# Gated linear attention and routed experts on one core: attention outputs computed turned, on halves and quarters of TensorE's array, and expert inputs turned on TensorE

## The chip, the cores and the metric

The kernel runs on one core of a Trainium2 chip. A core has five engines that work side by side, each through its own list of instructions in order: TensorE (PE: matrix products; its loads of the stationary operand are listed as PEld), VectorE (DVE), ScalarE (ACT), GpSimd (POOL) and SyncE (SP, which issues most DMAs here). TensorE writes to PSUM; VectorE and ScalarE read it from there. The metric is the device time of one execution in microseconds, as the median of several runs.

## The reference

Two layers follow each other. The first is a recurrence over 768 time steps, for 4 batches of 8 heads of width 48:

```python
state = alpha[:, :, t, :, None] * state + np.einsum('bhd,bhe->bhde', k[:, :, t], v[:, :, t])
y[:, :, t] = np.einsum('bhd,bhde->bhe', q[:, :, t], state)
```

(that is, the state decays by `alpha` in each key dimension, takes up the outer product of `k` and `v`, and is read by `q`). The 8 heads of a token laid side by side are its row `x` of 384 numbers, 3072 rows in all. The second layer sends each row to one of 8 experts:

```python
logits = x @ w_gate + modality_bias[modality_id]
e_idx = np.argmax(logits, axis=1)          # gate_w: softmax weight of that expert
h = np.maximum(x[mask] @ w1[e], 0.0)       # 384 -> 1024
out[mask] = gate_w[mask, None] * (h @ w2[e])
```

Everything is fp32.

## The kernel before

**Attention.** The tokens are cut into 24 pieces of 128 (6 per batch). One turn of the main loop (lines 666 to 705) is a step: it loads a piece, turns `alpha`, `k` and `q` on TensorE (`trans`, line 218: four 128x128 transposes for each, two heads padded to 64 rows each in one transpose), makes the running products of `alpha` forward and backward by two scans on VectorE (G, line 231; Fw, line 238), scales keys and queries with them (kh, qh: lines 254, 257), and then works in three stages of a software pipeline: `decay` of piece s, `scale` of piece s-1, `scores` of piece s-2, `combine` of piece s-3. `scores` (line 266) makes the 128x128 score blocks of 8 heads, each from 48 rows, into `sc`; ScalarE copies them out and GpSimd zeroes the upper triangle (line 271).

`combine` (lines 281 to 318) makes the output. The state that enters a piece is S; scaled, it is laid by ScalarE into `UB` (U), two heads of a pair on the diagonal of a 128x96 block with zeros elsewhere. The state's update `kv` (line 298) uses halves of the array: 64 output rows per head. The output `y` has tokens on the partitions and 384 columns. For each of the 4 head pairs there are three products with 96 columns: the turned queries qh (128 rows by 128 tokens, the stationary operand) with U (line 309), and for each of the two heads the turned scores (stationary) with `v`, padded by zero columns to the pair's 96 (line 312). That is 12 products a piece, 8 in the first piece of a batch, where there is no state. Each fp32 product is two records in the trace. ScalarE copies `y` to `xs` and SP sends it to the table `xd` in memory. `logits_pe` (line 320) then turns `xs` (three transposes, line 324), ScalarE copies the result to `xc`, and three products with 8 columns each (line 329) make the logits.

**Routing.** Groups of pieces are routed while the attention goes on (`route_group`, `route_early`), and the rest after the last piece (`route_end`, lines 496 to 540): a chain of small VectorE instructions with a few TensorE products between them, whose end is a table of row numbers by expert (lines 537, 445). Rows of one expert fill slots of 256.

**Experts.** `experts` (line 713) works through 12 full slots and, behind branches, a last part that in this data is one `half` (line 803). A slot gathers 256 rows of `xd` by index (GpSimd, line 577) and loads its expert's w1 and w2 (SP, lines 553, 555). To get more than the plain precision of the fast format, each operand is split in a rounded high part (ScalarE) and a low part that holds the rest (`split`, line 741: `eng.tensor_tensor` on VectorE, or for w2 of slot 0 and quarters 0 and 2 of w2 in every slot on GpSimd, line 772), and each product is three: high by high, low by high, high by low (lines 764 to 766 and 785 to 787). A slot is 72 products with 256 columns, 48 with 384. `prep` (line 721) turns the gathered rows: for slot 1 by six TensorE transposes, for the others by 16 32x32-block transposes on VectorE (line 737) into `xf`, from which ScalarE and VectorE make the high and low part (lines 738, 739). Slot 0's first layer (line 111) is done in plain fp32 between the routing's instructions.

What order each engine has is decided by a scheduler that simulates the program; `issue_after` holds some instructions back behind others. Few tiles limit it: `tr` has three PSUM buffers, `sc` two, `kv`, `y` and `rt` one.

Of the kernel before, what the change touches and what calls it, by code (L numbers as in the profile page):

```python
# [8 lines left out]
F32 = mybir.dt.float32  # L9
# [38 lines left out]
NTURN = 2  # L48
W2POOL = (0, 2)
# [7 lines left out]
def attention_moe(ctx: ExitStack, tc: tile.TileContext, q, k, v, alpha, mid, wg, mb, w1, w2, out):  # L57
# [28 lines left out]
    for i in range(NV):  # L86
        t = ac.tile([P, 2 * H + 1, D], F32, name=f"vt{i}")
        VT.append(t)
        pool.memset(t[:, 0::2], 0.0)
# [38 lines left out]
    def load(i, names="akqv"):  # L128
        b, c = divmod(i, NC)
        for n, t in (("a", alpha), ("k", k), ("q", q), ("v", v)):  # L130
            if n in names:
                dst = VT[i % NV][:, 1::2] if n == "v" else nat[n, i % NB][:, :, :D]
# [49 lines left out]
    pool.tensor_scalar(rev, iof[:, :E], -1.0, float(E), op0=ALU.mult, op1=ALU.add)  # L182
    ones = cp.tile([P, P], BF16, name="ones")
# [97 lines left out]
    def combine(i):  # L281
# [3 lines left out]
        if c > 0:  # L285
            S0 = st[i, "S"]
            A = st[i, "G"][:, 1::SEG].unsqueeze(2).broadcast_to([P, NP, D])
            t1 = sb.tile([P, NP, D], F32, name="t1")
            vec.tensor_tensor(t1, S0, A, op=ALU.mult)
            for g in range(2):  # L290
                r = slice(64 * g, 64 * g + 64)
                act.copy(U[r, :, g * D : (g + 1) * D], t1[r])
        if c < NC - 1:
            kn = st[i, "n"]
            kv = ps.tile([P, NP, D], F32, name="kv")
            for h in range(H):
                r = slice(64 * (h % 2), 64 * (h % 2) + 64)
                pe.matmul(kv[r, h // 2], kn[:, h // 2, r], vt[:, 2 * h + 1], start=True, stop=True)  # L298
# [6 lines left out]
        y = ps.tile([P, DM], F32, name="y")  # L305
        for j in range(NP):
            yj = y[:, 2 * D * j : 2 * D * (j + 1)]
            if c > 0:
                pe.matmul(yj, qh[:, j], U[:, j], start=True, stop=False)  # L309
            for g in range(2):  # L310
                z = 4 * j + 1 + g
                pe.matmul(  # L312
                    yj, sc[g][:, j], vt[:, z : z + 2].rearrange("p a b -> p (a b)"), start=(c == 0 and g == 0), stop=(g == 1)
                )
        xs = sb.tile([P, DM], F32, name="xs", bufs=4)
        act.copy(xs, y)
        sp.dma_start(xd[row(i) : row(i) + P, :], xs)
        st[i, "x"] = xs

    def logits_pe(i, xs, pl, after=None):  # L320
        xt = ps.tile([P, ND, P], F32, name="tr", bufs=3)
        with issue_after(after):
            for c in range(ND):
                mark["logitst"] = pe.transpose(xt[:, c], xs[:, c * P : (c + 1) * P], ident)  # L324
        xc = pl.tile([P, ND, P], F32, name="xc")
        mark["xc"] = act.copy(xc, xt)
        lp = ps.tile([P, E], F32, name="kv")
        for c in range(ND):
            mark["logits"] = pe.matmul(lp, xc[:, c], wgs[:, c], start=(c == 0), stop=(c == ND - 1))
# [336 lines left out]
    for s in range(NU + 4):  # L666
# [22 lines left out]
        if 0 <= s - 3 < NU:  # L689
# [3 lines left out]
            logits_pe(s - 3, st[s - 3, "x"], sb, ("step", ND - 1) if s - 3 == NU - 1 else None)  # L693
# [19 lines left out]
    def experts(ahead):  # L713
# [7 lines left out]
        def prep(i):  # L721
            x = xg[i % NX]
            xH, xL = XH[i % 2], XL[i % 2]
            if i < NTURN:
                for name, d0, d1 in (("kv", 0, 2), ("y", 2, 3)):
                    xp = ps.tile([P, d1 - d0, T], F32, name=name)
                    for d in range(d0, d1):
                        for u in range(2):
                            pe.transpose(xp[:, d - d0, u * P : (u + 1) * P], x[:, u, d * P : (d + 1) * P], ident)
                    act.copy(xH[:, d0:d1], xp)  # L730
                    vec.tensor_tensor(xL[:, d0:d1], xp, xH[:, d0:d1].bitcast(F32), op=ALU.subtract)
                return
            src = x.rearrange("p u (c a d) -> p a u c d", c=ND, a=4)
            dst = xf.rearrange("p c (u b t) -> p b u c t", u=2, b=4)
            for a in range(4):
                for b in range(4):
                    vec.transpose(dst[32 * a : 32 * (a + 1), b], src[32 * b : 32 * (b + 1), a])  # L737
            act.copy(xH, xf)
            vec.tensor_tensor(xL, xf, xH.bitcast(F32), op=ALU.subtract)

        def split(name, src, eng=vec):
# [3 lines left out]
            eng.tensor_tensor(lw, src, hi.bitcast(F32), op=ALU.subtract)  # L745
            return hi, lw

        def layer1(i):
# [5 lines left out]
            for j in range(4):  # L754
# [17 lines left out]
                w2s.append(split("w2", W2[:, 2 * j : 2 * j + 2], pool if plain or j in W2POOL else vec))  # L772
# [67 lines left out]
        def tail(i):  # L840
            if i < NS:
                with tc.If(ns > i):
                    with tc.If(nfl > i) as full:
                        ahead_of(i + 1)
                        slot(i)
# [65 lines left out]
```

## Time and profile before

| what | value |
|---|---|
| runs before | 463.2, 461.2, 463.09 us; median 463.09 us |
| the profiled execution's own time | 465.73 us |
| its span, first to last instruction | 464.0 us |
| mean granted TensorE clock in it | 0.954 |
| busy: PE, DVE, ACT, POOL | 410.2, 347.0, 229.1, 190.6 us |
| first to last transposes of a piece of `alpha` | 4.3 to 167 us |
| second layer of slot 0 begins | 219.8 us |
| last full slot ends, half slot begins | 432.6 us |
| last product of the half slot begins | 443.1 us |

A timeline row gives start, length, engine, line, operation, tiles (written <- read), shapes and how many; the length reaches to the end of the last one, which for TensorE includes its latency, so that the pace is read from one row's start to the next row's. A square bracket at the end is the engine's idle time before and what ended it. In a row of the windows view stands the stretch, its length, and for each engine busy time and number of instructions, then the granted clock (1.00 is full), the share of the DMA engines and GB/s.

### The profile page before, as it was taken

What the parts mean: (1) busy time and instruction counts of PE and PEld (TensorE: products, weight loads), DVE (VectorE), ACT (ScalarE), POOL (GpSimd) and SP (SyncE); (2) the same over time, 40 slices, a digit from 0 to 9 for tenths busy, and PEclk for the clock granted to TensorE, in tenths of its full rate; (3) what the DMA queues carried; (4) which work ended last, traced back from release to release, by engine and by line L of the source; (5) the groups of instructions that cost most, each with busy time, mean ns of one, the idle gap of its engine ahead of it and who ended that gap; (6) DMA issues with size and microseconds to landing.
All of it is one profiled execution on the core that took longest, in us unless ns stands there. A gap on an engine that the chain in (4) does not pass through costs nothing.

```text
span 464.0 us, 9508 instructions
## 1 busy us (share of the span) xinstructions
PE 410.2 (88%) x3432; PEld 390.1 (84%) x3432; DVE 347.0 (75%) x817; ACT 229.1 (49%) x419; POOL 190.6 (41%) x204
## 2 busy tenths in 40 slices
PE   4999999999999999987978797889999999999920
PEld 3889989898898888865968697899999999999910
DVE  7867777678769982458899999988978988932450
ACT  3565654656464445154645364536656665532410
POOL 9321212112121444043839775647657634720410
PEclk9999999999999999597999899989999999999975
DMA  8989764667465874000996564756586567472200
GB/s 162 198 182 198 170 140 102 134 141 165 89 144 106 290 249 172 19 17 9 383 340 192 203 216 160 270 188 209 188 302 210 184 250 264 134 223 99 65 18 5
DMA packets 134267, 78.76 MB, mean 170 GB/s; under 512 B 103489, under 2 KB 120958, under 8 KB 134200
## 3 DMA queue, kind: packets, MB, share of 16 engines
q1 hardware_dynamic: 129912, 67.70, 52.0%
q0 software_dynamic: 4288, 10.24, 6.4%
q8 instruction: 32, 0.52, 0.5%
q14 instruction: 35, 0.29, 0.2%
HBM read 68.48 MB, written 9.65 MB: 168 GB/s over the span
## 4 chain that ended last, share of the span: by engine, by line
PE 57%; DVE 23%; issue 8%; ACT 4%; POOL 3%; DMA 2%; SPq 0%; POOLq 0%; DVEq 0%; ACTq 0%
PE y L312 6%; PE sc L266 5%; PE sc L787 5%; PE sc L786 5%; PE sc L785 5%; PE tr L221 5%; PE tr L764 5%; PE tr L766 5%; PE tr L765 5%; DVE xf L737 4%; DVE G L231 3%; DVE Fw L238 3%; PE y L309 3%; PE kv L298 2%; PE tr L324 2%
## 5 line engine op out<-in xcount | busy, mean ns | idle before, releaser
L764 PE MATMUL tr<-xH,w1H 128*128 128x256 f32 x264 | 76.3, 289 | 12.8 <-DVE hL L770 10.6
L271 POOL TENSOR_SCALAR_AFFINE_SELECT scT<-scT 128x512 f32<-128x512 f32 x48 | 31.6, 680 | 123.2 <-ACT scT L270 123.2
L766 PE MATMUL tr<-xH,w1L 128*128 128x256 f32 x264 | 75.7, 287 | 0.0
L765 PE MATMUL tr<-xL,w1H 128*128 128x256 f32 x264 | 75.5, 286 | 0.0
L737 DVE STREAM_TRANSPOSE xf<-xg 32x192 f32<-32x192 f32 x192 | 71.0, 370 | 4.0 <-DMA xg<-xd,idx 1.2
L745 POOL TENSOR_TENSOR w2L<-w2r,w2H 128x768 fp32r<-128x768 f32 x26 | 48.2, 1862 | 61.6 <-ACT w2H L743 44.4
L787 PE MATMUL sc<-w2H,hL 128*128 128x384 f32 x192 | 61.7, 337 | 2.6 <-DVE hL L770 2.6
L764 PEld LDWEIGHTS tr<-xH,w1H 128*128 128x128 f32 x264 | 51.7, 196 | 14.4 <-issue 14.4
L785 PE MATMUL sc<-w2H,hH 128*128 128x384 f32 x192 | 63.6, 336 | 0.0
L786 PE MATMUL sc<-w2L,hH 128*128 128x384 f32 x192 | 63.3, 335 | 0.0
L312 PE MATMUL y<-vt,scT 128*128 128x96 f32 x384 | 60.5, 280 | 0.0
L745 DVE TENSOR_TENSOR w1L<-w1r,w1H 128x768 fp32r<-128x768 f32 x44 | 50.2, 1150 | 11.9 <-ACT w1H L743 11.7
L743 ACT CAST w1H<-w1r 128x768 fp32r<-128x768 f32 x44 | 36.3, 833 | 43.5 <-PE tr L765 27.1
L743 ACT CAST w2H<-w2r 128x768 fp32r<-128x768 f32 x52 | 42.7, 832 | 28.2 <-PE sc L787 16.2
L312 PEld LDWEIGHTS y<-vt,scT 128*128 128x128 f32 x384 | 52.3, 197 | 0.2
L765 PEld LDWEIGHTS tr<-xL,w1H 128*128 128x128 f32 x264 | 51.7, 196 | 0.0
L766 PEld LDWEIGHTS tr<-xH,w1L 128*128 128x128 f32 x264 | 51.6, 195 | 0.0
L577 POOL DMA_INDIRECT xg<-xd,idx x28 | 37.7, 1347 | 29.7 <-DVE xf L737 13.3
L770 DVE SCALAR_TENSOR_TENSOR hL<-tr,hH 128x512 fp32r<-128x512 f32 x48 | 32.8, 684 | 10.5 <-ACT hH L768 10.4
L787 PEld LDWEIGHTS sc<-w2H,hL 128*128 128x128 f32 x192 | 35.9, 188 | 3.8 <-DVE hL L770 3.8
L791 POOL DMA_INDIRECT out_dram<-os,odx x24 | 27.2, 1133 | 25.6 <-issue 11.0
L768 ACT ACTIVATE hH<-tr 128x512 fp32r<-128x512 f32 x48 | 28.5, 594 | 18.0 <-PE tr L766 9.4
(216 smaller groups left out, 851.0 us busy)
## 6 DMA issues: line engine op xcount, KB each, us to landing
w1r<-in_moe_w_dram SPq DMA_DIRECT2D x28, 768.0 KB
w2r<-in_moe_w_dram SPq DMA_DIRECT2D x28, 768.0 KB
nat_a<-in_alpha_dram SPq DMA_DIRECT2D x24, 192.0 KB
nat_k<-in_k_dram SPq DMA_DIRECT2D x24, 192.0 KB
nat_q<-in_q_dram SPq DMA_DIRECT2D x24, 192.0 KB
vt<-in_v_dram SPq DMA_DIRECT2D x24, 192.0 KB
xd<-xs SPq DMA_DIRECT2D x24, 192.0 KB
xg<-xd,idx POOLq DMA_INDIRECT x28
```

The source lines that it names most:

```text
L312: pe.matmul(yj, sc[g][:, j], vt[:, z : z + 2].rearrange("p a b -> p (a b)"), start=(c == 0 and g == 0), stop=(g == 1))
L577: pool.indirect_dma_start(xg[i % NX][:, u], None, xd[0:rows], ix, bounds_check=rows - 1, oob_is_err=False)
L737: vec.transpose(dst[32 * a : 32 * (a + 1), b], src[32 * b : 32 * (b + 1), a])
L743: act.copy(hi, src)
L745: eng.tensor_tensor(lw, src, hi.bitcast(F32), op=ALU.subtract)
L764: pe.matmul(hp[:, z], wH[:, d, fs], xH[:, d], start=(d == 0), stop=False)
L765: pe.matmul(hp[:, z], wH[:, d, fs], xL[:, d], start=False, stop=False)
L766: pe.matmul(hp[:, z], wL[:, d, fs], xH[:, d], start=False, stop=(d == ND - 1))
L770: vec.scalar_tensor_tensor(hL, hp, 0.0, hH.bitcast(F32), op0=ALU.max, op1=ALU.subtract)
L785: pe.matmul(op, hH[:, z, us], wH[:, z], start=(f == 0), stop=False)
L786: pe.matmul(op, hH[:, z, us], wL[:, z], start=False, stop=False)
L787: pe.matmul(op, hL[:, z, us], wH[:, z], start=False, stop=(f == NF - 1))
```

## The change

`y` is made turned. For each head pair and each of its two heads, a product has 64 output rows (half of the array's columns): U's 64 columns of that head, or the head's `v` padded from 48 to 64 columns, is now the stationary operand, and the queries or the scores (128 tokens) stream. A piece has 16 such products, 8 in a batch's first piece. ScalarE copies the turned output (512 columns) to `yt`. From `yt` two things are made: `rows` turns it back on TensorE (four transposes), ScalarE drops the padding, and SP sends it to `xd`; `logits` multiplies it with a padded `w_gate`, four products with 32 output rows each, on quarters of the array (the four head pairs' shares), ScalarE copies these, and one product with `sel8` adds the four shares. In the experts `prep` turns every slot's rows on TensorE and ScalarE and VectorE make the high and low parts straight from PSUM, and every low part of w2 is made on VectorE. The old `logits_pe` stays for a fallback path that isn't run.

```diff
-        t = ac.tile([P, 2 * H + 1, D], F32, name=f"vt{i}")
+        t = ac.tile([P, H, 64], F32, name=f"vt{i}")
...
+    wgp = ac.tile([P, NP, 32], F32, name="wgp")
+    pool.memset(wgp, 0.0)
+    for g in range(2):
+        sp.dma_start(wgp[64 * g : 64 * g + D, :, :E], wg.rearrange("(j g d) e -> g d j e", g=2, d=D)[g])
...
-        t = ac.tile([P, NP, 2 * D], F32, name=f"UB{i}")
+        t = ac.tile([P, NP, 2, 64], F32, name=f"UB{i}")
...
+    sel8 = ac.tile([P, E], F32, name="sel8")
+    pool.tensor_copy(sel8, ident[:, :E])
+    for j in range(1, NP):
+        pool.tensor_tensor(sel8, sel8, ident[:, 32 * j : 32 * j + E], op=ALU.add)
...
-        y = ps.tile([P, DM], F32, name="y")
+        y = ps.tile([P, NP, P], F32, name="y")
         for j in range(NP):
+            halves = [slice(64 * g, 64 * g + 64) for g in range(2)]
             if c > 0:
-                pe.matmul(yj, qh[:, j], U[:, j], start=True, stop=False)
-            for g in range(2):
-                z = 4 * j + 1 + g
-                pe.matmul(
-                    yj, sc[g][:, j], vt[:, z : z + 2].rearrange("p a b -> p (a b)"), start=(c == 0 and g == 0), stop=(g == 1)
+                for g, r in enumerate(halves):
+                    pe.matmul(y[r, j], U[:, j, g], qh[:, j], start=True, stop=False)
+            for g, r in enumerate(halves):
+                pe.matmul(y[r, j], vt[:, 2 * j + g], sc[g][:, j], start=(c == 0), stop=True)
+        yt = sb.tile([P, NP, P], F32, name="yt")
+        mark["yt"] = act.copy(yt, y)
...
+    def rows(i):
+        p = ps.tile([P, NP, P], F32, name="tr", bufs=3)
+        for j in range(NP):
+            pe.transpose(p[:, j], st[i, "y"][:, j], ident)
...
+        sp.dma_start(xd[row(i) : row(i) + P, :], xs)
+    def logits(i, after=None):
+        lt = ps.tile([P, P], F32, name="kv")
+        with issue_after(after):
+            for j in range(NP):
+                mark["logitst"] = pe.matmul(
+                    lt[32 * j : 32 * j + 32], wgp[:, j], st[i, "y"][:, j], start=True, stop=True
+                )
+        ls = sb.tile([P, P], F32, name="lts")
+        mark["xc"] = act.copy(ls, lt)
+        lp = ps.tile([P, E], F32, name="kv")
+        mark["logits"] = pe.matmul(lp, ls, sel8, start=True, stop=True)
...
-            for a in range(4):
-                for b in range(4):
-                    vec.transpose(dst[32 * a : 32 * (a + 1), b], src[32 * b : 32 * (b + 1), a])
-            act.copy(xH, xf)
-            vec.tensor_tensor(xL, xf, xH.bitcast(F32), op=ALU.subtract)
...
-                w2s.append(split("w2", W2[:, 2 * j : 2 * j + 2], pool if plain or j in W2POOL else vec))
+                w2s.append(split("w2", W2[:, 2 * j : 2 * j + 2]))
```

The scheduler orders the engines anew. TensorE in a step of the attention, before: L329 the logits, L221 transposes of a piece, L276 the turned keys, L309 and L312 the output, L298 the state, L266 the scores, L324 the logits' transposes.

```order
L329 MATMUL kv<-wgs,xc 128x8 x3
L221 MATMUL tr<-ident,nat_q_80 128x128 x4
L276 MATMUL tr<-ident,kh 128x128 x4
L312 MATMUL y<-vt_104,scT 128x96
L298 MATMUL kv<-vt_104,knat 64x48 x8
L266 MATMUL sc<-qh,kh 128x128 x8
L324 MATMUL tr<-ident,xs 128x128 x3
L221 MATMUL tr<-ident,nat_a_88 128x128 x4
L221 MATMUL tr<-ident,nat_k_84 128x128 x4
L309 MATMUL y<-UB_154,qh 128x96
```

The same place now: L341 the four shares of the logits, L228 transposes of a piece, L318 and L320 the output, L283 the turned keys, L347 the sum of the shares. Behind these rows follow three more output products, the scores, the state, and the transposes of `rows`.

```order
L341 MATMUL kv<-yt,wgp 32x128 x4
L228 MATMUL tr<-ident,nat_q_86 128x128 x4
L318 MATMUL y<-qh,UB_158 64x128
L283 MATMUL tr<-ident,kh 128x128 x4
L318 MATMUL y<-qh,UB_158 64x128
L320 MATMUL y<-scT,vt_106 64x128 x2
L318 MATMUL y<-qh,UB_158 64x128 x2
L320 MATMUL y<-scT,vt_106 64x128 x2
L318 MATMUL y<-qh,UB_158 64x128 x2
L320 MATMUL y<-scT,vt_106 64x128 x2
L318 MATMUL y<-qh,UB_158 64x128
L347 MATMUL kv<-sel_183,lts 128x8
```

The output's products (64 rows) are cut twice by products on the whole array (128 rows): by the turned keys and by the sum of the shares. Before, only the state and the scores left the whole array, and they stood side by side.

VectorE among the experts' slots, before (L737 turns a slot's rows, L739 its low part, L745 low parts of weights, L770 low part of the hidden layer):

```order
L739 TENSOR_TENSOR xL_2885<-xf,xH_2883 128x768
L745 TENSOR_TENSOR w2L<-w2r_113,w2H 128x768
L737 STREAM_TRANSPOSE xf<-xg_116 32x2x3x32 x16
L745 TENSOR_TENSOR w2L<-w2r_115,w2H 128x768
L745 TENSOR_TENSOR w1L<-w1r_114,w1H 128x768
L770 SCALAR_TENSOR_TENSOR hL<-tr,hH 128x512
```

And now (L761 the low part from PSUM, L769 weights, L794 hidden layer):

```order
L794 SCALAR_TENSOR_TENSOR hL<-tr,hH 128x512
L761 TENSOR_TENSOR xL_3118<-kv,xH_3116 128x512
L761 TENSOR_TENSOR xL_3118<-y,xH_3116 128x256
L769 TENSOR_TENSOR w1L<-w1r_114,w1H 128x768
L794 SCALAR_TENSOR_TENSOR hL<-tr,hH 128x512
L769 TENSOR_TENSOR w2L<-w2r_113,w2H 128x768 x2
L769 TENSOR_TENSOR w2L<-w2r_115,w2H 128x768 x2
```

The 16 block transposes are gone from VectorE's list, and four low parts of w2 stand there in each slot where two stood. On TensorE six transposes stand in each slot between the third and the fourth quarter of its first layer. GpSimd's list keeps its gathers and output writes and has no `w2L` any more.

More of the change, by code (lines that the diff above doesn't have):

```diff
@@ L47 @@
 AFLOOR = 1.0e-30
-NTURN = 2
-W2POOL = (0, 2)
 STEPS = (("key", 21), ("key0", 20), ("count", 9), ("rank", 8), ("logits", 6), ("logitst", 4))
@@ L131, in load @@
             if n in names:
-                dst = VT[i % NV][:, 1::2] if n == "v" else nat[n, i % NB][:, :, :D]
+                dst = VT[i % NV][:, :, :D] if n == "v" else nat[n, i % NB][:, :, :D]
                 sp.dma_start(dst, t[b, :, c * P : (c + 1) * P, :].rearrange("h t d -> t h d"))
@@ L291, in combine @@
                 r = slice(64 * g, 64 * g + 64)
-                act.copy(U[r, :, g * D : (g + 1) * D], t1[r])
+                act.copy(U[r, :, g, :D], t1[r])
         if c < NC - 1:
@@ L297, in combine @@
                 r = slice(64 * (h % 2), 64 * (h % 2) + 64)
-                pe.matmul(kv[r, h // 2], kn[:, h // 2, r], vt[:, 2 * h + 1], start=True, stop=True)
+                pe.matmul(kv[r, h // 2], kn[:, h // 2, r], vt[:, h, :D], start=True, stop=True)
             S1 = sb.tile([P, NP, D], F32, name="S")
@@ L315, in combine @@
[L315 to L320, printed above, removed]
+                for g, r in enumerate(halves):
[3 more added lines that the diff above has]
+        yt = sb.tile([P, NP, P], F32, name="yt")
@@ L321, in logits_pe @@
+    def logits_pe(i, xs, pl):
         xt = ps.tile([P, ND, P], F32, name="tr", bufs=3)
-        with issue_after(after):
-            for c in range(ND):
-                mark["logitst"] = pe.transpose(xt[:, c], xs[:, c * P : (c + 1) * P], ident)
+        for c in range(ND):
+            pe.transpose(xt[:, c], xs[:, c * P : (c + 1) * P], ident)
         xc = pl.tile([P, ND, P], F32, name="xc")
-        mark["xc"] = act.copy(xc, xt)
+        act.copy(xc, xt)
         lp = ps.tile([P, E], F32, name="kv")
@@ L328, in logits_pe @@
         for c in range(ND):
-            mark["logits"] = pe.matmul(lp, xc[:, c], wgs[:, c], start=(c == 0), stop=(c == ND - 1))
+            pe.matmul(lp, xc[:, c], wgs[:, c], start=(c == 0), stop=(c == ND - 1))
         vec.tensor_tensor(L[:, i], lp, bt[:, i], op=ALU.add)
@@ L692, in attention_moe @@
                 hp0 = first_steps()
-            logits_pe(s - 3, st[s - 3, "x"], sb, ("step", ND - 1) if s - 3 == NU - 1 else None)
+            logits(s - 3, ("step", ND - 1) if s - 3 == NU - 1 else None)
+            rows(s - 3)
             for after, t0, t1 in GROUPS:
@@ L723, in prep, with split @@
             xH, xL = XH[i % 2], XL[i % 2]
[L724 to L729, printed above, removed]
+            for name, d0, d1 in (("kv", 0, 2), ("y", 2, 3)):
+                xp = ps.tile([P, d1 - d0, T], F32, name=name)
+                for d in range(d0, d1):
+                    for u in range(2):
+                        pe.transpose(xp[:, d - d0, u * P : (u + 1) * P], x[:, u, d * P : (d + 1) * P], ident)
+                if i < NS0:
                     act.copy(xH[:, d0:d1], xp)
                     vec.tensor_tensor(xL[:, d0:d1], xp, xH[:, d0:d1].bitcast(F32), op=ALU.subtract)
-                return
-            src = x.rearrange("p u (c a d) -> p a u c d", c=ND, a=4)
-            dst = xf.rearrange("p c (u b t) -> p b u c t", u=2, b=4)
-            for a in range(4):
-                for b in range(4):
[L737 to L741, printed above, removed]
+                else:
+                    act.copy(xf[:, d0:d1], xp)
+        def split(name, src):
             hi = wp.tile(list(src.shape), F32R, name=name + "H")
@@ L844, in tail @@
                         ahead_of(i + 1)
+                        act.copy(XH[i % 2], xf)
+                        vec.tensor_tensor(XL[i % 2], xf, XH[i % 2].bitcast(F32), op=ALU.subtract)
                         slot(i)
```

10 lines of the change are left out of this document (7 added, 3 removed).

## The prediction

> **What bounds the kernel now.** I read busy time in windows first, then the order of time on TensorE (PE) inside a step, then who waits for whom. Two stretches of the experts, the first four full slots behind slot 0 and six later ones (start, length, then busy us of PE, its loads, DVE, ACT, POOL):
>
> ```profile
> 228.47:313.94 85.47, 72.28 (x480) 69.93 (x480) 80.78 (x138) 42.46 (x63) 53.40 (x40) 0.96 0.68 229
> 313.94:415.62 101.68, 101.68 (x721) 101.68 (x721) 84.09 (x150) 59.79 (x87) 58.02 (x43) 1.00 0.66 221
> ```
>
> A slot is 120 products, so the second row is six slots of 101.68 / 6 = 16.95 us, PE never idle: the pace PE can hold. Four slots at that pace are 67.8 us; the first row took 85.47. So 17.7 us are lost there, with DVE busy 80.78 of 85.47. DVE is what PE waits for:
>
> ```profile
> PE tr L764 <- DVE hL L770: 10.6, 4, 3.4
> ```
>
> Why DVE is late is seen on DVE and POOL side by side, here at 231:
>
> ```profile
> 230.00 0.96 DVE L745 TENSOR_TENSOR w2L<-w2r,w2H 128x768 fp32r<-128x768 f32 x1 [1.09 <-ACT w2H L743]
> 231.37 5.01 DVE L745 TENSOR_TENSOR w1L<-w1r,w1H 128x768 fp32r<-128x768 f32 x1 [0.40 <-ACT w1H L743]
> 236.31 1.88 DVE L737 STREAM_TRANSPOSE xf<-xg 32x192 f32<-32x192 f32 x5
> ...
> 231.89 3.67 POOL L745 TENSOR_TENSOR w2L<-w2r,w2H 128x768 fp32r<-128x768 f32 x2
> ```
>
> The same subtraction takes DVE 0.96 us alone and 5.01 us with two of POOL's beside it: while POOL reads both operands, DVE's instruction stands still. Over the run (min/median/max in ns):
>
> ```profile
> L745 DVE TENSOR_TENSOR w1L<-w1r,w1H x44: 946/955/5015, 221.6 to 403.9; 128x768 fp32r<-128x768 f32 x44
> L745 POOL TENSOR_TENSOR w2L<-w2r,w2H x26: 1809/1845/2252, 203.7 to 412.6; 128x768 fp32r<-128x768 f32 x26
> ...
> L737 DVE STREAM_TRANSPOSE xf<-xg x192: 355/370/377, 236.3 to 447.8; 32x192 f32<-32x192 f32 x192
> ```
>
> A step of the attention on PE, from scores to scores:
>
> ```profile
> 82.60 1.16 PE L266 MATMUL sc<-qh,kh 48*128 48x128 f32 x16
> 83.69 0.55 PE L324 MATMUL tr<-ident,xs 128*128 128x128 f32 x3
> 84.08 0.60 PE L221 MATMUL tr<-ident,nat_a 128*128 128x128 f32 x4
> 84.52 0.60 PE L221 MATMUL tr<-ident,nat_k 128*128 128x128 f32 x4
> 84.95 0.36 PE L309 MATMUL y<-UB,qh 128*128 128x96 f32 x2
> ...
> 87.38 0.76 PE L329 MATMUL kv<-wgs,xc 128*128 128x8 f32 x6
> 88.00 0.63 PE L221 MATMUL tr<-ident,nat_q 128*128 128x128 f32 x4
> ...
> 88.90 0.36 PE L312 MATMUL y<-vt,scT 128*128 128x96 f32 x2
> 89.24 0.67 PE L298 MATMUL kv<-vt,knat 128*64 128x48 f32 x16
> 89.84 1.16 PE L266 MATMUL sc<-qh,kh 48*128 48x128 f32 x16
> ```
>
> From 82.60 to 89.84 are 7.24 us without a gap: PE bounds the step. Starts give prices: a transpose (84.52 - 84.08) / 4 = 0.11; an output record (87.38 - 84.95) / 22 = 0.11; a logits record, with only 8 columns, (88.00 - 87.38) / 6 = 0.10, so that loading 128 columns costs 0.10 whatever streams; a score record, two of which run side by side, (83.69 - 82.60) / 16 = 0.068; a state record, in halves, (89.84 - 89.24) / 16 = 0.038.
>
> **The change, part by part.** The sum is made against the profiled execution, 465.73 us, which is 2.64 above the median of the runs shown, 463.09; I take the difference over to the median.
>
> *Output in halves.* Before, 24 records of 0.11 are 2.64 us. Now 16 products of two records each, paired by column halves as the state is, each streaming 128 columns as the scores do. No row shows 64 loaded columns with 128 streamed. From below the state's 0.038 gives 32 x 0.038 = 1.2 us, from above no overlap at all 32 x 0.11 = 3.5. Nearest are the scores, which stream as much: their 1.09 holds about 0.2 for leaving the paired mode (next part), so 0.9 / 16 = 0.056 a record, and 32 x 0.056 = 1.79. Gain 0.85.
>
> *Changes of mode.* One score product once stood alone between transposes:
>
> ```profile
> 181.30 0.55 PE L324 MATMUL tr<-ident,xs 128*128 128x128 f32 x3
> 181.78 0.48 PE L266 MATMUL sc<-qh,kh 48*128 48x128 f32 x2
> 182.19 0.66 PE L120 MATMUL sc<-ident,xg 128*128 128x128 f32 x4
> ```
>
> Three transposes and two records are 0.55 us at 0.11; they took 182.19 - 181.30 = 0.89. Going over to part of the array and back costs 0.34 (I allow 0.2 to 0.4). The new order has three more such excursions in a usual step: one for the quarter products, and two because the turned keys and the sum of the shares cut the output's block. That is 3 x 0.34 = 1.02 given back.
>
> *Logits and rows.* Six records (0.62) go. Four quarter products come, 8 records, between 0.22 (four at once) and 0.88 (one by one); I take 0.25, the row of halves being nearest, and one full product, 0.22: gain 0.15. `rows` has one transpose more: 0.11.
>
> A usual step: -0.85 + 1.02 - 0.15 + 0.11 = +0.13, 7.4 us instead of 7.24. In a batch's first piece 16 records become 16 paired ones and often one excursion less is added: about -0.5 or better, and its neighbours gain too. Priced row by row over the whole order to the first plain-fp32 product of slot 0, PE's list comes to 169.6 us before and 164.5 now. But near batch changes DVE's scans, not PE, set the pace, so not all of it arrives: -3 (from -8 to +6).
>
> What lies beside: ScalarE copies 512 columns instead of 384 and one small piece more, but is busy 4.09 of 7.24 us in such a step; `rows` sends `xd` somewhat later, hidden by 20 us of routing before a gather reads it (if not, slot 2's rows are late); two small DMAs stand in SP's queue before the third piece's loads, and GpSimd's longer `sel8` is paid by its shorter zeroing of `vt`. I leave the start at zero, with 1 us either way.
>
> *Routing.* POOL's subtractions for slot 0 stand beside the last routing chain on DVE, and stretch it:
>
> ```profile
> 203.73 7.13 POOL L745 TENSOR_TENSOR w2L<-w2r,w2H 128x768 fp32r<-128x768 f32 x4 [17.01 <-DVE m L368]
> ...
> 205.57 1.78 DVE L389 SCALAR_TENSOR_TENSOR hj<-thr,r,onh 128x23 f32<-128x23 f32 x1
> ...
> 209.32 1.55 DVE L392 SCALAR_TENSOR_TENSOR hi<-m,hr 128x2 f16<-128x2 f32 x1
> ```
>
> In other groups, with POOL quiet, L392 takes 0.16:
>
> ```profile
> L392 DVE SCALAR_TENSOR_TENSOR hi<-m,hr 128x6 f16<-128x6 f32 x2 | 0.3, 166 | 0.1
> ```
>
> L392 alone loses 1.4 and L389, with 23 columns about as short, 1.4 or so twice; with two others 6 us or so go. But the four subtractions now stand in DVE's list between the same instructions: 4 x 0.955 = 3.8 come back. Then PE's plain-fp32 products must fit too. I take -1.5 (from -6 to +2).
>
> *Experts.* DVE loses 16 x 0.37 = 5.9 us of transposes in a slot and every stall behind POOL (1.85 each), and gets two subtractions, 1.9. Its backlog goes: the 17.7 us come back, less a rest for the first slot, whose low parts still wait for weights; I take 2 for that rest (0 to 6). Against it six transposes stand on PE in slots 1 to 11: 11 x 6 x 0.11 = 7.3 us, bare cost, since PE has no idle time there. Sum -17.7 + 2 + 7.3 = -8.4 (from -10.5 to -4). The rows' splits read PSUM, for which DVE has no longer work than from SBUF:
>
> ```profile
> L731 DVE TENSOR_TENSOR xL<-kv,xH 128x512 fp32r<-128x512 f32 x1 | 0.7, 673 | 0.0
> ```
>
> DVE then has about 8 x 0.955 + 4 x 0.68 + 1.1 = 11.5 us in a slot of 17.6.
>
> *End.* The last transposes on DVE go, but the last output leaves as early as before, and POOL ends after it:
>
> ```profile
> 443.48 0.58 ACT L830 ACTIVATE os<-sc,gg 128x384 f32<-128x384 f32 x1 [3.44 <-PE sc L828]
> 444.34 1.03 POOL L832 DMA_INDIRECT out_dram<-os,odx  x1 [2.34 <-POOLq L843]
> ...
> 449.04 0.96 DVE L739 TENSOR_TENSOR xL<-xf,xH 128x768 fp32r<-128x768 f32 x1 [0.90 <-ACT xH L738]
> ```
>
> Zero, at best the 4 us by which DVE ends later. The split moved into the branch for a full slot isn't run: the last part is a half.
>
> Sum: -3 - 1.5 - 8.4 + 0 = -13, so 452.8 for such an execution and 450 for the median.
>
> **The rivals.**
>
> *Loads don't overlap in halves* (the slower side). If the array's halves load and stream in turn, a pair of output records takes 0.05 (64 columns) + 0.11 = 0.16 instead of 0.112. The order has 352 output products, each half of two pairs: 352 x 0.048 = +17, so 467. It decides from 0.149 a pair on, where 352 x 0.037 eats the 13 us. Against it: a state pair, loading 0.05 and streaming 0.04, would take 0.09, and takes 0.075 with the changes of mode in it. The Trainium skill, TensorE: Matmul & The Clock Gate, Part 3, says that a load overlaps running products only if their row groups differ, which in halves by columns they don't; the state's row speaks against it. 5%.
>
> *The clock drops.* The new PE work has more transposes. If these don't count as activity, the clock is halved in steps rich in them; a stretch at half clock costs half of its length.
>
> ```profile
> 63.26:66.67 3.41, 3.11 (x38) 2.58 (x37) 3.27 (x13) 2.13 (x5) 0.00 (x0) 1.00 0.73 164
> 66.67:70.09 3.42, 3.42 (x38) 2.99 (x37) 3.38 (x11) 1.88 (x4) 0.36 (x1) 1.00 0.77 151
> 186.14:196.38 10.24, 9.67 (x53) 8.44 (x52) 4.50 (x31) 1.66 (x4) 0.57 (x1) 0.50 0.06 20
> ```
>
> In the first of these TensorE ran, among others:
>
> ```profile
> 63.65 0.63 PE L221 MATMUL tr<-ident,nat_q 128*128 128x128 f32 x4
> 64.12 0.60 PE L276 MATMUL tr<-ident,kh 128*128 128x128 f32 x4
> 64.56 0.49 PE L324 MATMUL tr<-ident,xs 128*128 128x128 f32 x3
> ```
>
> That stretch holds 15 transposes in all and little else that streams, and the clock stays 1.00 behind it; it fell to 0.50 at 186, after waits. If one stretch of 3.4 us in each step were halved, 24 x 1.7 = +41: 491. The Trainium skill, TensorE: Matmul & The Clock Gate, Part 4, says that transposes don't count as busy the way products do; these rows disagree. 3%.
>
> *The experts' loss stays.* If weights or order, not DVE, hold the first slots, 17.7 remain and 7.3 are added: 450 + 15.7 = 466. The DMA share there is 0.68, as in the slots that run full (0.66), which speaks against it. 5% for all, 10% for about half: 458.
>
> *More arrives.* Routing gains its 6 and the attention its 8: 450 - 4.5 - 5 = 440. 12%.
>
> My forecast: 65%.
>
> **How the numbers follow.** The likeliest is 450. The terms' bounds together with half a lost expert gain and the better rival give 437 to 461. About 0.5% (2.3 us) is what a measurement of this kernel can tell from no change. Faster than 460.8: forecast, better rival and half loss, 0.87. Slower than 465.4: the three rivals above that, less their milder forms, 0.08. Between: 0.05.
>
> **What would show it.** In the new profile: usual steps of 7.3 to 7.5 us on PE; two output records starting together every 0.11; slots of 17.6 us from the first on, PE busy throughout; w1L near 0.95 at most; no waits of PE on `hL`. Wrong would be output pairs at 0.16, granted clock under 1 in the attention, or gaps on PE behind slot 0 of more than 6 us in all.

## The result, and the profile after

The changed kernel takes 449.02 us (median of 4 runs, 446.06 to 449.69), the kernel before 462.14 (4 runs): ratio 0.9706, 95% interval 0.9651 to 0.976. The forecast was 450.0.

A second profile of the kernel before was taken for the comparison, since its first execution (465.73 us) lay above its median and its second (458.79) below. The five places are bounded by instructions on the path: the last score block of the attention, slot 0's first product of the second layer, the half slot's first product, the start of its output scale on ScalarE, the last instruction.

| place, us | before, 1st profile | before, 2nd profile | changed | changed less mean of before | forecast |
|---|---|---|---|---|---|
| start to last score block | 182.0 | 182.3 | 176.6 | -5.5 | -3 |
| to slot 0's second layer (routing) | 37.8 | 32.2 | 33.4 | -1.6 | -1.5 |
| to the half slot (full slots) | 212.8 | 211.7 | 202.3 | -10.0 | -8.4 |
| half slot to its output scale | 10.9 | 10.0 | 15.8 | +5.3 | 0 |
| to the end | 20.5 | 20.7 | 19.3 | -1.3 | 0 |
| span | 464.0 | 457.0 | 447.4 | -13.1 | -13 |
| the execution's own time | 465.73 | 458.79 | 449.16 | | |

So the sum came out right, but the attention and the full slots gained more than forecast, and the loss in the half slot was not in the sum at all. The routing's -1.6 rests on the first profile: against the second alone that place is 1.2 us longer, not shorter. The runs below say more of it.

A usual step of the attention on TensorE now, from scores to scores:

```profile
79.70 1.16 PE L273 MATMUL sc<-qh,kh 48*128 48x128 f32 x16
80.79 0.67 PE L305 MATMUL kv<-vt,knat 128*64 128x48 f32 x16
81.39 0.66 PE L329 MATMUL tr<-ident,yt 128*128 128x128 f32 x4
81.88 0.60 PE L228 MATMUL tr<-ident,nat_a 128*128 128x128 f32 x4
82.32 0.60 PE L228 MATMUL tr<-ident,nat_k 128*128 128x128 f32 x4
82.85 0.42 PE L341 MATMUL kv<-yt,wgp 128*32 128x128 f32 x8
83.21 0.66 PE L228 MATMUL tr<-ident,nat_q 128*128 128x128 f32 x4
83.79 0.43 PE L318 MATMUL y<-qh,UB 128*64 128x128 f32 x2
84.16 0.66 PE L283 MATMUL tr<-ident,kh 128*128 128x128 f32 x4
84.74 0.32 PE L318 MATMUL y<-qh,UB 128*64 128x128 f32 x1
84.75 0.32 PE L320 MATMUL y<-scT,vt 128*64 128x128 f32 x1
84.90 0.27 PE L318 MATMUL y<-qh,UB 128*64 128x128 f32 x1
84.91 0.38 PE L320 MATMUL y<-scT,vt 128*64 128x128 f32 x2
85.02 0.27 PE L318 MATMUL y<-qh,UB 128*64 128x128 f32 x1
...
85.98 0.39 PE L347 MATMUL kv<-sel,lts 128*128 128x8 f32 x2
...
87.10 1.16 PE L273 MATMUL sc<-qh,kh 48*128 48x128 f32 x16
```

87.10 - 79.70 = 7.40, as worked out. The two products at 84.74 and 84.75 start together: the halves run side by side. So do the two at 84.90 and 84.91, and the next pair (the second of 84.91's two, and 85.02) follows 0.11 later. The two cuts at L283 and L347 are there. That the step came out to the hundredth is partly luck, for two misses in it cancel: the quarter products take 83.21 - 82.85 = 0.36 with their changes of mode (forecast 0.25 + 0.34 = 0.59), and the output block with its two cuts takes 87.10 - 83.79 = 3.31, less 0.66 for the six full-width records in it, 2.65 (forecast 1.79 + 0.68 = 2.47).

The granted clock is 1.00 in this step, but not in the whole attention. Once TensorE waited 1.34 us for scaled queries, and the next 3.4 us ran at half clock:

```profile
149.77:153.18 3.41, 2.07 (x35) 1.75 (x35) 3.41 (x16) 1.23 (x4) 2.99 (x2) 1.00 1.04 391
153.18:156.59 3.41, 3.41 (x25) 2.37 (x25) 1.26 (x12) 2.75 (x7) 1.50 (x3) 0.50 1.06 385
```

Neither profile of the kernel before has such a stretch between its first 17 us and its last scores. At half clock 3.4 us of TensorE's work are 1.7 us of loss at most.

The full slots now, four from the first layer of slot 1 on and six later ones:

```profile
219.06:289.14 70.08, 70.08 (x503) 70.06 (x502) 45.49 (x61) 42.21 (x66) 31.69 (x28) 1.00 0.78 271
289.14:394.70 105.56, 105.56 (x757) 105.56 (x756) 64.24 (x82) 60.48 (x93) 37.16 (x33) 1.00 0.66 218
```

105.56 / 6 = 17.59 and 70.08 / 4 = 17.52: no slot loses anything, TensorE is never idle, VectorE is busy 45.49 of 70.08 where it was busy 80.78 of 85.47.

The half slot, which the forecast had left alone (of TensorE, GpSimd and ScalarE):

```profile
412.32 5.52 PE L838 MATMUL tr<-xf,w1r 128*128 128x128 f32 x48
...
417.18 1.68 POOL L606 DMA_INDIRECT xg<-xd,idx  x1 [0.73 <-DVE hL L842]
...
421.66 0.30 PE L758 MATMUL kv<-ident,xg 128*128 128x128 f32 x1 [3.82 <-DMA xg<-xd,idx]
...
428.12 0.58 ACT L854 ACTIVATE os<-sc,gg 128x384 f32<-128x384 f32 x1 [9.60 <-PE sc L852]
```

L758 turns the rows of the next part, which in this data is never run. It stands on TensorE ahead of the half's own second layer, and waits 3.82 us for a gather that GpSimd issued from 417.18 on. Behind that wait the clock is halved for 3.4 us:

```profile
417.85:421.63 3.78, 0.00 (x0) 0.00 (x1) 1.55 (x3) 0.60 (x1) 3.03 (x3) 1.00 0.30 78
...
422.83:426.24 3.41, 3.41 (x13) 3.31 (x12) 0.00 (x0) 0.00 (x0) 0.00 (x0) 0.50 0.06 14
```

3.8 of wait, 1.7 of half clock (half of 3.4) and 0.66 for six transposes make 6.2. The place is 6.0 longer than in the run below where the transposes stand behind the output.

### The profile page after: what moved, and what is told of

Its sections match the earlier page's. It is cut to its first block, busy times and chain, and to the rows that moved or that the text cites. A ratio compares the mean times of both kernels' runs of the same rounds, so it can differ in the third digit from the quotient of the medians.

```text
span 447.4 us, 10022 instructions
## 1 busy us (share of the span) xinstructions
PE 406.1 (91%) x3784; PEld 369.5 (83%) x3784; DVE 280.3 (63%) x659; ACT 238.3 (53%) x455; POOL 135.6 (30%) x183
## 5 line engine op out<-in xcount | busy, mean ns | idle before, releaser
L769 DVE TENSOR_TENSOR w2L<-w2r,w2H 128x768 fp32r<-128x768 f32 x52 | 49.3, 956 | 51.8 <-ACT w2H L767 50.5
L790 PE MATMUL tr<-xH,w1L 128*128 128x256 f32 x264 | 74.6, 283 | 0.0
L815 POOL DMA_INDIRECT out_dram<-os,odx x24 | 25.9, 1078 | 103.0 <-ACT os L813 70.7
L769 DVE TENSOR_TENSOR w1L<-w1r,w1H 128x768 fp32r<-128x768 f32 x44 | 41.8, 957 | 22.2 <-ACT w1H L767 17.7
L790 PEld LDWEIGHTS tr<-xH,w1L 128*128 128x128 f32 x264 | 50.4, 191 | 0.0
L606 POOL DMA_INDIRECT xg<-xd,idx x28 | 35.0, 1251 | 43.8 <-DVE vals L475 29.4
L320 PE MATMUL y<-scT,vt 128*64 128x128 f32 x384 | 44.4, 279 | 0.0
L318 PE MATMUL y<-qh,UB 128*64 128x128 f32 x320 | 41.0, 282 | 0.4 <-ACT UB L299 0.4
L794 DVE SCALAR_TENSOR_TENSOR hL<-tr,hH 128x512 fp32r<-128x512 f32 x48 | 32.9, 685 | 13.0 <-ACT hH L792 13.0
L611 POOL DMA_INDIRECT gg<-gd,idx x28 | 31.9, 1138 | 18.9 <-DMA gd<-gs 9.1
L809 PEld LDWEIGHTS sc<-w2H,hH 128*128 128x128 f32 x192 | 36.3, 189 | 0.0
```

Source lines behind the costliest of these rows:

```text
L318: pe.matmul(y[r, j], U[:, j, g], qh[:, j], start=True, stop=False)
L320: pe.matmul(y[r, j], vt[:, 2 * j + g], sc[g][:, j], start=(c == 0), stop=True)
L606: pool.indirect_dma_start(xg[i % NX][:, u], None, xd[0:rows], ix, bounds_check=rows - 1, oob_is_err=False)
L769: vec.tensor_tensor(lw, src, hi.bitcast(F32), op=ALU.subtract)
L790: pe.matmul(hp[:, z], wL[:, d, fs], xH[:, d], start=False, stop=(d == ND - 1))
L794: vec.scalar_tensor_tensor(hL, hp, 0.0, hH.bitcast(F32), op0=ALU.max, op1=ALU.subtract)
```

## The experiments

All times are medians; each ratio is to runs of the kernel before on the same chip, with its 95% interval. "Changed" is 449.02 us, ratio 0.9706.

**The two parts apart.** First the changed attention with the experts of before:

```diff
-            vec.tensor_tensor(lw, src, hi.bitcast(F32), op=ALU.subtract)
+            eng.tensor_tensor(lw, src, hi.bitcast(F32), op=ALU.subtract)
...
-                w2s.append(split("w2", W2[:, 2 * j : 2 * j + 2]))
+                w2s.append(split("w2", W2[:, 2 * j : 2 * j + 2], pool if plain or j in W2POOL else vec))
...
+            if i < NTURN:
...
+            for a in range(4):
+                for b in range(4):
+                    vec.transpose(dst[32 * a : 32 * (a + 1), b], src[32 * b : 32 * (b + 1), a])
```

> The attention of the changed kernel with the experts of the kernel before (turns on VectorE, quarters 0 and 2 of w2's low parts on GpSimd). If the two parts add, as the forecast has it: the attention brings 3 to 4 us, the routing chain stays stretched by GpSimd, so 458 to 460 us (the kernel before 462). If the output in halves were what starts the experts early enough for all else: 450 to 453. If the attention brings nothing: 462.

Measured: 455.35 us, 0.9872 (0.9829 to 0.9916), some 6 us less than before; the last score block at 176.6 us as in the changed kernel. More than expected, since the attention gains 5.5 and not 3 to 4, and the full slots take 210.3 us, 1.4 to 2.5 less than before with the same code; why is not shown. The half slot takes 10.0.

The other half is the same diff the other way round on the kernel before: the changed experts with the old attention.

> The experts of the changed kernel with the attention of the kernel before. If the parts add: 449 + 3 to 4, so 452 to 453 us, slots of 17.6 us from the first on, the routing chain short again, and the half slot waiting 4 us for a gather as in the changed kernel. If the experts gain only because they start earlier behind the new attention: 457 or more.

Measured: 453.32 us, 0.982 (0.9776 to 0.9864), as expected for parts that add: 0.9872 x 0.982 = 0.9694 against 0.9706 measured for both. Its profiled execution took 459.55 us; no place of it is compared.

**What the full slots lost.** The low parts back on GpSimd, the rows still turned on TensorE (the first four changed lines above):

> The changed kernel, but the low parts of w2 that GpSimd made before (all of slot 0, quarters 0 and 2 of the others) are on GpSimd again; rows are still turned on TensorE. If GpSimd's subtractions stop VectorE wherever both run, the chain of the last routing is stretched again and the first slots lose: 452 to 456 us, with single VectorE instructions at 1.3 to 5 us. VectorE then has some 10 us of work and 4 of stalls in a slot of 17.6, so the later slots keep their pace. If only the amount of VectorE's work counted: 448 to 450, since it has less of it.

Measured: 452.32 us, 0.9823 (0.9772 to 0.9874). That is in the range of the first expectation, but the first slots don't lose (the table below). The 3.1 us over the changed kernel in the profiles lie in the routing (36.8 instead of 33.4) and at the end (21.5 instead of 19.3); the half slot is shorter (13.1 instead of 15.8). And the reverse, the rows turned on VectorE, no low part on GpSimd:

```diff
+            if i >= 2:
...
+                for a in range(4):
+                    for b in range(4):
+                        vec.transpose(dst[32 * a : 32 * (a + 1), b], src[32 * b : 32 * (b + 1), a])
```

> The changed kernel, but from slot 2 on rows are turned by 16 block transposes on VectorE as before; every low part of w2 stays on VectorE, none on GpSimd. VectorE's list for a slot is 8 x 0.957 + 4 x 0.69 + 16 x 0.37 + 0.96 = 17.3 us against 16.95 on TensorE. If stalls behind GpSimd were the loss: slots of 17.3 to 17.6 us, and the half slot waits for no gather on TensorE: 441 to 447 us. If the amount of VectorE's work was the loss: slots of 18 to 19 us at first, TensorE waiting for hL: 455 or more.

Measured: 447.34 us, 0.9694 (0.965 to 0.9738). Neither expectation of this run holds as it was put: the time is near the first, the slots are those of the second. The full slots take 208.6 us, 6.3 more than in the changed kernel; what makes up for it is the half slot (9.8 instead of 15.8), where TensorE waits for no gather, and the routing (31.2 instead of 33.4). VectorE and the slots in this run, w1L's times (min/median/max in ns), then what TensorE waits for:

```profile
L779 DVE TENSOR_TENSOR w1L<-w1r,w1H x44: 948/951/960, 209.5 to 389.2; 128x768 fp32r<-128x768 f32 x44
```

```profile
PE tr L798 <- DVE hL L804: 8.7, 5, 2.3
```

Not one subtraction is stopped here, and TensorE still waits for `hL`, with VectorE busy nearly all the time from 225 us on:

```profile
225.00:310.00 85.00, 78.72 (x525) 77.37 (x526) 82.08 (x150) 46.20 (x68) 40.18 (x33) 0.96 0.73 244
```

With GpSimd's subtractions back and the rows on TensorE it is the other way round: VectorE's instructions are stopped again (w2L, min/median/max),

```profile
L769 DVE TENSOR_TENSOR w2L<-w2r,w2H x26: 943/1348/3339, 219.3 to 421.5; 128x768 fp32r<-128x768 f32 x26
```

and the full slots take 202.4 us, as in the changed kernel (202.3). The four cases side by side, full slots in us:

| | rows turned on VectorE | rows turned on TensorE |
|---|---|---|
| low parts of w2 partly on GpSimd | 210.3 (old attention: 212.8 and 211.7) | 202.4 |
| all on VectorE | 208.6 | 202.3 |

With the new attention in all four, taking the turns from VectorE brings 7.9 us with GpSimd's subtractions there and 6.3 without them. Taking the subtractions from GpSimd brings 1.7 as long as the turns are on VectorE, and 0.1 when they are not. Against the kernel before, with its old attention, the two figures with the other cause in place are 9.3 to 10.4 (turns) and 3.1 to 4.2 (subtractions). So the 5.9 us of turns a slot were most of what overloaded VectorE. The 1.7 to 4.2 are net of the two subtractions that VectorE takes over in each slot, so they are not the price of the stalls themselves.

**Half of the turns on VectorE**, to see how near its limit it is (on the kernel of the next paragraph; 16 block transposes for one half of the rows, three transposes on TensorE for the other):

```diff
+            if 2 <= i < NS0:
+                src = x[:, 0].rearrange("p (c a d) -> p a c d", c=ND, a=4)
...
+                for d in range(ND):
+                    pe.transpose(xp[:, d], x[:, 1, d * P : (d + 1) * P], ident)
```

> The kernel with the half slot's output first (439.8 us); from slot 2 on one half of a slot's rows is turned by 16 smaller block transposes on VectorE, the other by three transposes on TensorE. TensorE needs 16.95 + 0.33 = 17.3 us for a slot instead of 17.62, VectorE about 8 x 0.957 + 4 x 0.69 + 16 x 0.25 + 1.3 = 15.7. If VectorE keeps up with a margin of 1.6 us: 10 slots x 0.33 less, 436 to 437. If VectorE falls behind in the first slots, as with all rows turned there (slots of 19 to 21 us): 440 or more.

Measured: 443.99 us, 0.9608 (0.9561 to 0.9654); its base came out at 0.9545 and 0.9579. Early slots, then late ones:

```profile
225.00:280.00 55.00, 51.69 (x363) 50.73 (x363) 53.59 (x115) 31.41 (x50) 28.12 (x24) 1.00 0.75 255
280.00:380.00 100.00, 100.00 (x710) 100.00 (x709) 83.62 (x161) 59.19 (x93) 38.06 (x33) 1.00 0.66 228
```

From 280 us on the slots take the 17.3 us expected. Before that VectorE is busy 53.59 of 55 and TensorE idle 3.3: in the first slots VectorE is behind, and a margin of 1.6 us a slot is too little to catch up at once. That it is the routing that leaves it behind is likely, but not shown. Full slots in all: 202.9 us, no gain.

**The half slot's output first.** The transposes of the next part stand behind the half's last product:

```diff
-                pe.matmul(op, hL[:, f % 4], wH[:, f % 2], start=False, stop=(f == NF - 1))
+                done = pe.matmul(op, hL[:, f % 4], wH[:, f % 2], start=False, stop=(f == NF - 1))
...
-                        half(i)
+                        done = half(i)
                         if i + 1 < NS:
-                            prep(i + 1)
+                            with tc.issue_after(done.ins):
+                                prep(i + 1)
```

> The changed kernel; in the branch of a half slot the transposes of the next part's rows stand behind the half's last product instead of ahead of its second layer. In the changed kernel TensorE stands there for 3.8 us until a gather lands, and runs at half clock behind it; from the half's first product to its output scale are 15.8 us where 10.9 were before. If the end hangs on that output, 4.9 us go: 444 us. If the end is set by the transfers of earlier slots or by GpSimd's queue: 448 to 449.

Measured: 439.81 us, 0.9545 (0.9508 to 0.9582). TensorE and ScalarE in its half slot:

```profile
410.01 5.52 PE L838 MATMUL tr<-xf,w1r 128*128 128x128 f32 x48
...
419.56 0.27 PE L758 MATMUL kv<-ident,xg 128*128 128x128 f32 x1
419.81 0.58 ACT L854 ACTIVATE os<-sc,gg 128x384 f32<-128x384 f32 x1 [3.59 <-PE sc L852]
420.50 0.55 PE L758 MATMUL kv<-ident,xg 128*128 128x128 f32 x3 [0.67 <-DMA xg<-xd,idx]
```

419.81 - 410.01 = 9.8 instead of 15.8, and from there to the end 19.6 (19.3 in the changed kernel): the end does hang on this output. That is 6.0; the time fell by 9.2. To see whether the rest belongs to it, the same kernel was run once more:

> The kernel with the half slot's output first once more. Its first runs gave 439.81 us, 9.2 less than the changed kernel, where its profile accounts for 6.0 in the half slot; three kernels built on it came out 2 to 4 us above it in another call, though two of them lack nothing in their profiles. If the 3 us beyond the half slot were chance: 441 to 443, ratio near 0.958. If they belong to the kernel: 438 to 440.5, ratio near 0.954.

Measured: 443.1 us (441.75 without the longest of its six runs, 446.68), 0.9579 (0.9511 to 0.9647), half slot 9.8 again. So the rest did not come again and is taken for chance. This kernel is faster than the kernel before, and than the changed one by 1.3% (0.9579 against 0.9706) to 1.7% (0.9545); its intervals lie below the changed kernel's (0.9651 to 0.976).

**GpSimd beside the routing.** On that kernel, slot 0's four low parts alone back on GpSimd:

```diff
-                w2s.append(split("w2", W2[:, 2 * j : 2 * j + 2]))
+                w2s.append(split("w2", W2[:, 2 * j : 2 * j + 2], pool if plain else vec))
```

> The kernel with the half slot's output ahead of the next part's transposes (439.8 us, ratio to the kernel before 0.9545), but slot 0's four low parts of w2 on GpSimd again, all others on VectorE. If these four stretch the last routing chain on VectorE by more than the 3.8 us that they cost there: from the last scores to slot 0's second layer 35 to 37 us instead of 31 to 33, so 442 to 444. If the routing's gain was chance or came from the attention: 438 to 441.

Measured: 444.26 us, 0.9616 (0.9567 to 0.9664). VectorE and GpSimd in its last routing chain:

```profile
195.54 7.13 POOL L769 TENSOR_TENSOR w2L<-w2r,w2H 128x768 fp32r<-128x768 f32 x4 [13.62 <-DVE rj L408]
...
195.58 1.82 DVE L418 SCALAR_TENSOR_TENSOR hj<-thr,r,onh 128x23 f32<-128x23 f32 x1
...
197.44 1.73 DVE L418 SCALAR_TENSOR_TENSOR hj<-thr,r,onh 128x23 f32<-128x23 f32 x1
...
199.37 1.55 DVE L421 SCALAR_TENSOR_TENSOR hi<-m,hr 128x2 f16<-128x2 f32 x1
...
201.18 1.77 DVE L424 TENSOR_SCALAR OL<-ioh,lo,tok 128x128 f16<-128x128 f16 x2
202.87 0.15 DVE L540 TENSOR_TENSOR runs<-nn 128x8 f32<-128x8 f32 x1
```

And the same place without them, in the kernel that this run is built on (VectorE alone):

```profile
194.30 0.24 DVE L418 SCALAR_TENSOR_TENSOR hj<-thr,r,onh 128x23 f32<-128x23 f32 x1
...
194.46 0.95 DVE L769 TENSOR_TENSOR w2L<-w2r,w2H 128x768 fp32r<-128x768 f32 x1
195.34 0.24 DVE L418 SCALAR_TENSOR_TENSOR hj<-thr,r,onh 128x23 f32<-128x23 f32 x1
...
195.77 1.82 DVE L769 TENSOR_TENSOR w2L<-w2r,w2H 128x768 fp32r<-128x768 f32 x2
197.50 0.15 DVE L421 SCALAR_TENSOR_TENSOR hi<-m,hr 128x2 f16<-128x2 f32 x1
...
199.88 0.16 DVE L540 TENSOR_TENSOR runs<-nn 128x8 f32<-128x8 f32 x1
```

The stalled instructions take 1.55 to 1.82 instead of 0.15 to 0.24; from the first `hj` to `runs` are 7.3 us against 5.6, though the subtractions stand in the second chain. From the last maximum (L394) to the slots' table of experts (L554) are 14.3 us here, 13.1 and 13.4 in the two profiles without; 15.1 and 14.6 in the kernel before. In the two other profiles that have GpSimd's subtractions beside the changed attention (the two parts apart, and the low parts back on GpSimd) it is 15.8. So GpSimd beside the chain costs 0.9 to 2.7 us net.

The whole place, from the last scores to slot 0's second layer, is 34.3 us here, 31.6 and 31.8 without. Over all profiles with the changed attention in this order it is 34.3, 35.6 and 36.8 with GpSimd's subtractions and 31.2 to 33.4 without (five profiles): 3.4 apart in the mean, as this run's expectation had it. What the chain doesn't explain of it isn't shown; these profiles differ also in the clock granted there.

**Neighbours in the same half.** The output products in another order:

```diff
-        for j in range(NP):
-            halves = [slice(64 * g, 64 * g + 64) for g in range(2)]
-            if c > 0:
-                for g, r in enumerate(halves):
+        for g in range(2):
+            r = slice(64 * g, 64 * g + 64)
+            for j in range(NP):
+                if c > 0:
                     pe.matmul(y[r, j], U[:, j, g], qh[:, j], start=True, stop=False)
-            for g, r in enumerate(halves):
                 pe.matmul(y[r, j], vt[:, 2 * j + g], sc[g][:, j], start=(c == 0), stop=True)
```

> The changed kernel; the output products of a piece in another order: all of the first half of the columns, then all of the second, so that neighbours use the same half; as many changes of mode. If the gain of the output in halves is that neighbours in different halves run at the same time, 704 records of 0.055 us become 0.11: steps longer by 1.7 us, in all by 30 to 38 us: 480 to 487. If a record in halves costs 0.055 by itself: 449.

Measured: 469.67 us, 1.0188 (1.0137 to 1.024), slower than the kernel before. TensorE:

```profile
101.24 0.38 PE L319 MATMUL y<-scT,vt 128*64 128x128 f32 x2
101.45 0.38 PE L318 MATMUL y<-qh,UB 128*64 128x128 f32 x2
101.67 0.38 PE L319 MATMUL y<-scT,vt 128*64 128x128 f32 x2
```

Two records start every 0.215, four did in the changed kernel: 0.108 a record, as for the full width. The whole gain of the halves is that neighbours in different halves run together. Usual steps take 8.93 us, 1.53 more (expected 1.7); the attention is 19.8 longer and not 30, because other steps had fewer of these records or room for them: one beside a change of batch, in which TensorE had waited 1.15 us for VectorE, went from 8.63 only to 8.93.

**Fewer changes of mode.** The turned keys ahead of the output block, the sum of the shares behind it:

```diff
+        with issue_after("turned"):
             for j in range(NP):
...
+    def add_shares(i):
+        lp = ps.tile([P, E], F32, name="kv")
+        with issue_after("y"):
+            mark["logits"] = pe.matmul(lp, st[i, "ls"], sel8, start=True, stop=True)
```

> The changed kernel; each piece's turned keys are issued ahead of its output block, and the sum of the logits' shares behind the next one's, so that the 16 output products mostly stand together: 139 changes of mode on TensorE's list ahead of the experts instead of 200. At 0.1 to 0.17 us a change 6 to 10 us of TensorE's list go, of which VectorE lets perhaps half through: 444 to 447 us, usual steps of 6.8 us instead of 7.4. If changes of mode cost nothing, or VectorE sets the pace: 449.

Measured: 444.24 us, 0.9637 (0.9602 to 0.9672). The time is in the range expected, but not for that reason: its attention ends at 177.6, no earlier. In the first batch TensorE now waited 2.2 us for ScalarE's copy of the output (`yt`) and ran 3.4 us at half clock behind that (27.60 to 31.02, granted 0.50), and the fourth score block began at 34.7 instead of 28.9. What the run gained lies elsewhere: in the routing (30.0 instead of 33.4) and in the half slot (13.6 instead of 15.8). The twelve steps from the sixth score block to the eighteenth took 84.9 us against 86.1. So the new order was kept from the second batch on, with the half slot's output first:

> The kernel with the half slot's output first (439.8 us), and from the second batch on the output block in one piece, as in the run with fewer changes of mode, whose first batch was held up by another order of the start. 154 changes of mode instead of 200. In that run twelve steps of the attention took 84.9 us against 86.1: if that holds, 1.5 to 3 us go, 437 to 438.5. If VectorE takes all back: 440.

Measured: 441.59 us, 0.9578 (0.9521 to 0.9635). TensorE where the block is whole:

```profile
97.17 0.60 PE L283 MATMUL tr<-ident,kh 128*128 128x128 f32 x4
97.70 0.44 PE L319 MATMUL y<-qh,UB 128*64 128x128 f32 x4
...
99.28 0.39 PE L321 MATMUL y<-scT,vt 128*64 128x128 f32 x4
99.59 0.39 PE L352 MATMUL kv<-sel,lts 128*128 128x8 f32 x2
99.91 1.16 PE L273 MATMUL sc<-qh,kh 48*128 48x128 f32 x16
```

32 records take 99.59 - 97.70 = 1.89. In the changed kernel's step the same 32, with both cuts, take 87.10 - 83.79 less 6 whole records (0.66), 2.65: 0.38 a cut. The attention of this run ends at 173.8 us, 1.7 to 2.6 earlier than its base's. Its median lies between its base's two (439.81 and 443.1), so whether it is faster stays open.

**The kernel before once more.**

> The kernel before once more, for a second profile of it. Its first profiled execution took 465.73 us, the median of its runs is 462.14. If the difference lies in one place, the second profile shows it, and the change is then compared place by place with an ordinary execution: first layer-2 product of slot 0 at 217 to 220 us, 12 full slots, half slot 10.9 us.

Measured: 458.79 us. Its second layer begins at 214.5 instead of 219.8, earlier than the 217 to 220 expected, and its half slot takes 10.0 instead of 10.9; the other places agree within 1.1 us. Most of the difference is in the routing (37.8 and 32.2), and goes with the clock: over that place the granted clock is 0.78 in the first profile and 0.95 in the second, which is 8.3 and 1.6 us lost if TensorE had set the pace throughout. One stretch of it, the first profile, then the second:

```profile
190.00:196.40 6.40, 5.83 (x20) 4.87 (x20) 2.24 (x20) 1.66 (x4) 0.00 (x0) 0.50 0.09 32
```

```profile
190.00:196.40 6.40, 5.83 (x47) 5.44 (x45) 0.55 (x3) 0.96 (x2) 0.00 (x0) 1.00 0.09 32
```

## Why the prediction was right, and where it was wrong

The direction and the size held, and so did the mechanism of the output in halves, of the changes of mode and, in the main, of the experts; the step on the end failed. That the sum met 449 to a microsecond is luck: the attention and the full slots gave 4 us more than forecast, and the half slot with the end took 4 back.

- *Output in halves* (1.79 us for 32 records): 1.89 where the block is whole. The rival that loads don't overlap in halves is refuted: it asked for 0.16 a pair, 0.11 was measured. The Trainium skill, TensorE: Matmul & The Clock Gate, Part 3, has the sentence that a load overlaps running products only when their row groups differ, which is this rival's mechanism. The runs differ from it: pairs of products with the same rows and different columns share 0.11, and only neighbours in the same columns follow each other.
- *Changes of mode* (0.34 each way and back): 0.38. The usual step: 7.4 forecast, 7.40 measured.
- *The attention's sum*: TensorE's list, priced row by row, had said 5.1; the forecast took 3, because "near batch changes DVE's scans, not PE, set the pace". 5.5 came. The discount was the mis-sized term: from 4 us to the last scores TensorE is idle 8.9 us in the first profile of the kernel before and 7.9 in the changed kernel, so waits took back nothing of the shorter list. That holds even with the 1.7 us that the stretch at half clock may have cost.
- *Routing* (1.5): the chain is 1.2 to 1.7 shorter than in the kernel before, and 0.9 to 2.7 shorter with the changed attention on both sides. Its place varies by 5.6 us between two executions of the kernel before, so that no pair of profiles could have shown it. The eight profiles with the changed attention put it at 3.4 in the mean, so the term was rather too small.
- *Experts* (8.4): 9.4 to 10.5 between the kernels, 8.0 with the new attention on both sides (210.3 to 202.3). The rest of 2 us for the first slot wasn't there, and 17.59 us a slot were forecast as 17.6. The reason given was half wrong: the stalls behind GpSimd, put first, were the small part; the transposes on VectorE, put beside them, were most of it. The rival that this loss stays is refuted by every run with the rows on TensorE.
- *End* ("the last output leaves as early as before"): this step failed: the last output left 5.3 us later behind the half slot's first product than in the mean of the two profiles before, 6.0 later than with the step undone. It asked what the removed transposes on VectorE set free, and not where the added ones on TensorE would stand in the half's branch. On VectorE they had waited for their gather with nothing behind them; on TensorE the half's second layer is behind them. With that undone (439.81 and 443.1) the forecast would have been 7 to 10 us too high.
- *The clock* stayed at 1.00 in the steps of the attention with more transposes in them, but for one stretch of 3.4 us at 0.50, behind a wait. So the rival as it was put, one such stretch in each step, is refuted; one of 24 came. In the changed kernel each later stretch at half clock, too, follows 3.4 us in which TensorE was idle for 1.3 us or more.

## What to carry to other kernels

When a step moves to another engine, list for each place where it is issued, branches included, what stands behind it there and what it waits for: a prefetch that waits harmlessly on an idle engine blocks the result on a busy one. Two causes that make the same engine late are told apart by putting back one at a time; here the eye-catching stalls were the smaller part of the loss, and the plain amount of work the larger. Products on half of the array's columns pay when their neighbours use the other half and stand together; each interruption by a full-width product costs about seven records' time.

## What the runs showed of the hardware

- Two products in different column halves start 0.01 us apart or together and share 0.11 us; two in the same half take 0.108 each, as much as at full width.
- Leaving column halves for a full-width product and coming back costs 0.38 us beyond the products.
- The same program, in the same 6.4 us of its routing, ran at half clock in one execution and at full clock in another (granted 0.50 with 20 products, 1.00 with 47; TensorE busy 5.83 of 6.40 us in both): part of a spread of 5.3 us in where the experts begin. The Trainium skill, TensorE: Matmul & The Clock Gate, Part 1, says that the window by which activity is judged runs freely, so that the loss differs from run to run; these rows fit that, but what set the two executions apart is not shown.
- A wait of 3.8 us on TensorE was followed, 1.2 us after its end, by 3.4 us at a granted clock of 0.50; one of 1.34 us by 3.4 us at 0.50 as well, 1.3 us after its end.
